# Written order for three engines in the last pass of a decode kernel's backward, with the stages that need new loads at the end of an item

## The chip, the core and the metric

The kernel runs on one core of one Trainium2 chip. The metric is the device time of one execution in microseconds (us); lower is better. The kernel before takes 2007.58 us, the median of three runs (2006.96 to 2015.45). The profiled execution has a span of 2011.2 us.

## The reference

Two layers are applied twice to a single token `x` of 1024 numbers, and the kernel returns the output and the gradients of everything (`jax.vjp`):

```python
x = x + A(layernorm(x), k_cache, v_cache, wq, wo)     # attention with a cache
x = x + B(layernorm(x), w1, b1, w2, b2)               # relu(h)**2 in between
x = x + A(layernorm(x), k_cache, v_cache, wq, wo)     # the same weights and caches
x = x + B(layernorm(x), w1, b1, w2, b2)
# in A: q = x @ wq in 32 heads; 8 heads share one of 4 groups of k and v, each 65536 x 128
#       p = softmax(q k^T / sqrt(128)); o = p v; o @ wo
```

All inputs and outputs are bfloat16. The caches are 67 MB each for k and for v, and their gradients, which sum over both uses of A, are as large. A gradient of k or v at one position is a sum of 16 outer products (8 heads, 2 layers).

## The kernel before, in words

The work goes through the caches in four passes: forward of the first attention, forward of the second, backward of the second (these three are `attn_fwd`, `attn_fwd` and `attn_bwd3`), and the last one, `attn_bwd4` (L1263), which does the backward of the first attention and writes the gradients of k and v for both. Between the passes lie the dense layers.

**Items and stages.** A pass walks over 256 items; an item is 8 columns of 128 cache rows in one of the 4 groups, in the order of `ITEMS[3]` (all items of a group, then the next group). Blocks of J = 32 columns, that is of 4 items and 1 MB, are what one DMA loads or stores. `pipeline` (L825) is a software pipeline: in step i it calls, for each entry of a list of stages, that stage's function for the item that is due by the stage's lag, then one step of background work (`bg.step`). The stages of the last pass are: `vT` takes a block of v from its load (`kv8`, which emits the load on SyncE where it is first asked for) and transposes 8 tiles on TensorE into a PSUM tile `ps_tr`, which `evac` (L150) copies to `kt`; the first seven blocks were kept transposed from the pass before. `vS` multiplies these by the output's gradient into `ps_sc` and, at the end of a block, VectorE multiplies that by the stored exponentials into `X` (L1367). `eIn` copies the exponentials of a block on GpSimd; `eT` and `xT` transpose the exponentials and `X` of a block (L1334). `dV8` and `dK8` make the gradients of v and k: `outer16` (L1382) has two products of two matmuls each into a PSUM tile `ps_gg` (L1390), evacuates each to a slot in `arena` (by `evac`, on ScalarE at L161 or VectorE at L164), and stores the full block from GpSimd's queue (L1396). `k8` takes a block of k from its load and accumulates the gradient of q in `ps_acc` (L1421).

**Buffers.** In this pass PSUM holds 2 buffers of `ps_tr`, 1 of `ps_sc`, 2 of `ps_gg` and 1 of `ps_acc`. SBUF has 20 slots of one block each (`arena`); 8 hold the exponentials of the four groups at the start and come free two by two, as a group ends. A load or a staging tile takes a slot when the code asks for it, and waits on the chip for that slot's last user, often a store.

**Background.** `Background` (L762) steps generators: `g_outer` and `g_outer_wide` make the weight gradients, each step one product into `ps_gg` (`rank2`, L1467) or its rows (`rows2`, L1452); `g_rowdots` (L562) loads two slabs of wo or wq, yields "wait" for eight steps, and then multiplies 8 rows on VectorE, one a step (L583), with a sum on ScalarE (L572).

**What sets the order.** The order in which Python emits instructions need not be the order on an engine. Outside of a region marked `tc.manual_schedule`, a scheduler reorders each engine's instructions by a simulation of when their inputs are ready. Inside such a region the named engines keep the written order; SyncE and GpSimd are still ordered by the scheduler. `ORDERED` (L981) names TensorE, VectorE and ScalarE, and the first three passes are already in such regions; the last one is not. `keep_in_program_order` pins a single instruction behind all that was emitted for its engine before it.

**The end.** At the last item `k8` calls `on4` (L1742), whose `else` branch does what is left: the product with wq (`PRE["rows"].run()`), the last layernorm's backward and the last weight gradient. Ten steps before the end `fill4` (L1761) transposes the last slabs of wq and drains the background.

Of the kernel before, what the change touches and what calls it, by code (L numbers as in the profile page):

```python
# [20 lines left out]
def kernel(  # L21
# [540 lines left out]
    def g_rowdots(slab_it, nk, vcol, nj, finish, name):  # L562
        n = nj * P
        y = vec.tile([P, nk], F32, name=name)
        nc.gpsimd.memset(y[:], 0.0)
        vbc = None
        due = None
        steps = 8 if PS["pass4"] else WAIT_STEPS

        def total(t, kc):  # L570
            def f():
                nc.scalar.activation(out=t[:, :], in_=t[:, :], func=ACTF.Copy, accum_out=y[:, kc:kc + 1])  # L572
            return f
        for kc, slab in slab_it:
            if vbc is None:
                vbc = yield from g_bcast_vec(vcol, nj)
                for _ in range(steps - WAIT_STEPS + 1):
                    yield "wait"
            elif kc % 4 == 0:
                for _ in range(steps):  # L580
                    yield "wait"
            t = mvs.tile([P, n], BF, name="mv_t", tag="mv_t", bufs=2)
            nc.vector.tensor_tensor(out=t[:, :], in0=slab, in1=vbc[:, :], op=ALU.mult)  # L583
            add_load(dve=0.1 + n * 0.00054, act=0.42 + n * 0.00083)
            if due is not None:
                due()
            due = total(t, kc)
            yield
        due()
        yield  # L590
        r = finish(y[:, :])
        if r is not None:
            yield from r
        yield


    class Rows:
# [227 lines left out]
    def pipeline(items, stages, bg, end=(), holds=(), lead=None):  # L825

        def due(lag):
            at = {}
            for k, it in enumerate(items):
                at.setdefault(k + lag + LEAD if lead is None or lag >= 0 else k + ~lag + lead(k), []).append(it)  # L830
            return at
        LEAD = 0 if lead is None else lead(len(items))
        when = [due(l) for _, l in stages]
        maxlag = max(l for _, l in stages) + LEAD
        for i in range(len(items) + maxlag):
            NOW["i"] = i
            NOW["wide"] = NOW["pairs"]
            for at, k in holds:
                if i == at:
                    hold(k)  # L840
            tasks(i - 0.5)
            for n, (fn, lag) in enumerate(stages):
                for it in when[n].get(i, ()):
                    fn(*it)
                if n == 0:
                    tasks(i)
            bg.step(max(0, i - LEAD))
            NOW["wide"] = False
            NOW["step"] += 1
            for before, fn in end:  # L850
                if i == len(items) + maxlag - before:
                    fn()
        while TASKS:
            k = min(TASKS)
            NOW["i"] = int(k + 0.5)
            tasks(k)
# [406 lines left out]
    def attn_bwd4(p, La, Lb, on_group, bg, stack, end=()):  # L1263
# [172 lines left out]
        for b in range(V_LEAD * 8 // J // 2):  # L1436
            nexts.append(("k",) + items[(b + 2) * J // 8])
            nexts.append(("v",) + items[(b + NKEEP[2]) * J // 8])
        pipeline(items, [(vT, ~0), (vS, ~TLEAD), (eIn, 0), (eT, TLEAD), (dV8, DV_LAG), (xT, DK_LAG - 1), (dK8, DK_LAG), (k8, B4_LAG)], bg,
                 end, lead=V_SHIFT)  # L1440

# [300 lines left out]
    def on4(g):  # L1742
        if g != lastg[3]:
            bg.add(g_dn(L1, dn1, g, g == firstg[3]))
            bg.normal.append(gwq(g))
        else:
            next(PRE["gwq"])
            PRE["rows"].run()
            next(PRE["gwq"])
            dxn1 = ln_bwd(dn1[:], L1["n"], L1["rstd"])  # L1750
            dx0 = tmp.tile([P, DC], F32, name="dx0")
            nc.vector.tensor_tensor(out=dx0[:], in0=dx1[:], in1=dxn1[:], op=ALU.add)
            col_to_dram(dx0, D, out_1.rearrange("a b d -> (a b d)"))
            run(PRE["gwq"])

    def last_v():

# [3 lines left out]
    def fill4():  # L1761
# [5 lines left out]
                                  lastg[3] * 1024)  # L1767
        next(PRE["gwq"])
    attn_bwd4(3, L1, L3, on4, bg, b4, [(12 + B4_LAG, last_v), (20, pre_load("wq4", lambda: wq_slabs(lastg[3], 2))), (10, fill4)])
    b4.close()  # L1770
    ps4_stack.close()

# [29 lines left out]
```

## Time and profile before

| | before |
|---|---|
| time, median of 3 | 2007.58 us |
| span of the profiled execution | 2011.2 us |
| TensorE busy | 1627.2 us (81%) |
| VectorE busy | 1171.7 us (58%) |
| ScalarE busy | 1045.1 us (52%) |
| GpSimd busy | 142.9 us (7%) |
| moved by DMA | 794.98 MB, mean 395 GB/s |
| granted TensorE clock, mean | 0.892 |

The last pass runs from about 1212 us to the end. Shares of busy time are means over stages with different limits; the busy time of TensorE is of pipelined matmuls with modelled ends, so it says little about how close TensorE is to its limit. The DMA share, by contrast, is near 1.00 in most of the span: a window with a full DMA share can't be shortened by anything but moving fewer bytes or moving them at a better rate. What ends a wait is named by the profile from semaphore events ("<-").

### The profile page before, as it was taken

The page shows a single profiled execution, that of the slowest core. Times are in us where ns is not written, and L with a number is a line of the kernel's source. Part 1 is how long each engine was busy: PE and PEld are TensorE (multiplying, and loading weights), DVE is VectorE, ACT ScalarE, POOL GpSimd, SP SyncE. Part 2 cuts the span into 40 slices and gives each one's busy share as a digit, 9 for nine tenths or more (in the row PEclk, how much of TensorE's full clock was granted, in tenths as well). Part 3 has the DMA queues.
Part 4 walks back from the last instruction along what each step waited for, and adds up shares of the span by engine and source line. Part 5 has one row for each costly group of instructions (what it writes and reads, how often), then busy time and mean ns, then how long its engine had stood idle before and what let it go on. Part 6 is the DMA issues. An engine that isn't in the chain of part 4 may idle for free. (4 is left out here: it accounts for less than half of the span.)

```text
span 2011.2 us, 67084 instructions
## 1 busy us (share of the span) xinstructions
PE 1627.2 (81%) x30228; PEld 1319.5 (66%) x30228; DVE 1171.7 (58%) x2426; ACT 1045.1 (52%) x1608; POOL 142.9 (7%) x332
## 2 busy tenths in 40 slices
PE   6877788687877777878787888788789799977887
PEld 6877777687777776767777785455455465644554
DVE  5645555255545544435454477656677677866775
ACT  3534344253433453426354365656678576756765
POOL 0000000000000000000000001111111111111211
PEclk9989999699999998899888999878898877888996
DMA  9999999999999998899999987998999999999996
GB/s 390 421 424 420 424 424 402 395 405 420 425 420 424 425 391 335 356 421 424 417 420 412 394 311 284 360 377 350 394 418 424 423 411 370 418 423 388 424 404 243
DMA packets 101037, 794.98 MB, mean 395 GB/s; under 512 B 9472, under 2 KB 9486, under 8 KB 37134
## 3 DMA queue, kind: packets, MB, share of 16 engines
q1 hardware_dynamic: 76670, 624.99, 76.2%
q0 software_dynamic: 24080, 165.70, 20.0%
q8 instruction: 236, 3.87, 0.8%
q14 instruction: 51, 0.42, 0.1%
HBM read 624.96 MB, written 165.69 MB: 393 GB/s over the span
## 5 line engine op out<-in xcount | busy, mean ns | idle before, releaser
L164 DVE COPY kt<-ps_tr 128x1024 bf16<-128x1024 bf16 x724 | 496.4, 688 | 489.8 <-PE ps_tr L1007 252.6
L161 ACT CAST arena<-ps_gg 128x1024 bf16<-128x1024 f32 x457 | 446.9, 1012 | 234.2 <-PE ps_gg L1390 161.6
L1007 PE MATMUL ps_tr<-ident_b,arena 128*128 128x128 bf16 x3840 | 306.9, 224 | 45.6 <-DMA arena<-in_A_k_cache_dram 33.3
L161 ACT COPY kt<-ps_tr 128x1024 bf16<-128x1024 bf16 x164 | 170.9, 1047 | 191.7 <-PE ps_tr L1199 113.5
L1007 PEld LDWEIGHTS <-arena 128*128 128x128 bf16 x3840 | 231.4, 100 | 54.1 <-DMA arena<-in_A_k_cache_dram 36.5
L1109 PE MATMUL ps_acc<-arena 128*128 128x64 bf16 (+4 forms) x4096 | 203.8, 195 | 67.5 <-DMA arena<-in_A_v_cache_dram 53.8
L164 DVE CAST arena<-ps_gg 128x1024 bf16<-128x1024 f32 (+2 forms) x186 | 222.2, 1195 | 61.5 <-PE ps_gg L1390 32.4
L1390 PE MATMUL ps_gg<-GG,xt 64*128 64x512 bf16 x1024 | 221.5, 433 | 21.5 <-ACT arena L161 13.1
L1319 PE MATMUL ps_tr<-ident_b,arena 128*128 128x128 bf16 x1824 | 186.6, 240 | 39.1 <-DMA arena<-in_A_v_cache_dram 37.7
L1109 PEld LDWEIGHTS <-arena 128*128 128x128 bf16 x4096 | 157.7, 100 | 73.2 <-DMA arena<-in_A_v_cache_dram 57.4
L1090 ACT ACTIVATE arena<-S_sb,L_negm 128x128 bf16<-128x128 f32 x256 | 165.5, 1003 | 62.4 <-DVE L_negm L1075 62.4
L1199 PE MATMUL ps_tr<-ident_b,arena 128*128 128x128 bf16 x1920 | 157.9, 229 | 43.8 <-DMA arena<-in_A_v_cache_dram 41.6
L1025 PE MATMUL ps_sc<-L_qpad,kt 128*128 128x64 bf16 (+7 forms) x3584 | 181.7, 193 | 14.2 <-ACT kt L161 6.6
L1319 PEld LDWEIGHTS <-arena 128*128 128x128 bf16 x1824 | 123.9, 107 | 98.0 <-issue 56.1
L1025 PEld LDWEIGHTS <-kt 128*128 128x128 bf16 x3584 | 151.2, 100 | 19.3 <-ACT kt L161 8.9
L1199 PEld LDWEIGHTS <-arena 128*128 128x128 bf16 x1920 | 119.8, 103 | 49.3 <-DMA arena<-in_A_v_cache_dram 44.7
L1421 PEld LDWEIGHTS <-arena 128*128 128x128 bf16 x2048 | 97.8, 105 | 73.4 <-issue 47.5
L1090 ACT ACTIVATION_READ_ACCUMULATOR arena<-S_sb,L_negm 128x1 f32 x256 | 128.1, 500 | 0.0
L1350 PEld LDWEIGHTS <-kt 128*128 128x128 bf16 x1824 | 86.5, 104 | 56.6 <-issue 55.7
L1350 PE MATMUL ps_sc<-DOB,kt 128*128 128x64 bf16 (+3 forms) x1824 | 119.1, 201 | 0.0
L1244 PE MATMUL ps_acc<-dsT,arena 128*128 128x64 bf16 (+7 forms) x2048 | 103.8, 195 | 14.0 <-DMA arena<-in_A_k_cache_dram 10.4
L1421 PE MATMUL ps_acc<-X,arena 128*128 128x64 bf16 (+3 forms) x1536 | 99.6, 203 | 15.7 <-DMA arena<-in_A_k_cache_dram 15.7
(292 smaller groups left out, 2160.7 us busy)
## 6 DMA issues: line engine op xcount, KB each, us to landing
arena<-in_A_k_cache_dram SPq DMA_DIRECT2D x86, 2048.0 KB, 21.3
arena<-in_A_v_cache_dram SPq DMA_DIRECT2D x83, 2048.0 KB, 21.1
out_dram<-arena POOLq DMA_DIRECT2D x149, 1024.0 KB, 10.4
arena<-in_A_v_cache_dram SPq DMA_DIRECT2D x76, 1024.0 KB, 11.7
arena<-in_A_k_cache_dram SPq DMA_DIRECT2D x76, 1024.0 KB, 11.4
arena<-in_B_w_dram SPq DMA_DIRECT2D x32, 896.0 KB, 7.9
arena<-in_A_wo_dram SPq DMA_DIRECT2D x22, 1024.0 KB, 13.6
arena<-in_A_wq_dram SPq DMA_DIRECT2D x20, 1024.0 KB, 14.5
```

The costliest lines, as they stand in the source:

```text
L161: nc.scalar.copy(out=out, in_=in_)
L164: nc.vector.tensor_copy(out=out, in_=in_)
L1007: nc.tensor.transpose(pt[:, i, :], kb8[:, i, :], ident_b[:, :])
L1025: nc.tensor.matmul(state["ps_s"][:, s:s + w, :].rearrange("p a b -> p (a b)"), lhsT=kt[:, i, :], rhs=L["qpad"][:, g, 0:w, :].rearrange("p ...
L1090: nc.scalar.activation(out=E(p, g, c0, SU)[:, :, h], in_=S[:, h, :], func=ACTF.Exp, bias=L["negm"][:, g, su, h:h + 1], scale=SCALE, accum_ ...
L1109: nc.tensor.matmul(ps_o[:, 0:w, :], lhsT=vb8[:, i, :], rhs=E(p, g, c, w), start=(c % SU == 0), stop=(c % SU == SU - 1), skip_group_check=True)
L1199: nc.tensor.transpose(pt[:, i, :], vb8[:, i, :], ident_b[:, :])
L1244: nc.tensor.matmul(ps_dq[:, 0:w, :].rearrange("p a b -> p (a b)"), lhsT=kb8[:, i, :], rhs=dsT[:, s:s + w, :].rearrange("p a b -> p (a b)") ...
L1319: nc.tensor.transpose(pt[:, i, :], vb8[:, i, :], ident_b[:, :])
L1350: nc.tensor.matmul(state["ps_dp"][:, s:s + w, :].rearrange("p a b -> p (a b)"), lhsT=vt[:, i, :], rhs=DOB[:, g, 0:w, :].rearrange("p a b - ...
L1390: nc.tensor.matmul(pg[:, 512 * h:512 * h + 512], lhsT=xt[64 * h:64 * h + 64, j1 // 8 + m, :], rhs=gg[64 * h:64 * h + 64, :, :].rearrange(" ...
L1421: nc.tensor.matmul(ps_dq[:, 0:w, :].rearrange("p a b -> p (a b)"), lhsT=kb8[:, i, :], rhs=X[:, s:s + w, :].rearrange("p a b -> p (a b)"), ...
```

## The change

The last pass is put into the written order on TensorE, VectorE and ScalarE, as the other passes are. The list of stages is reordered: those that need no new load come first in an item, and `vT` and `k8`, which need one, come last. (The list's first entry was also the point after which a step's tasks run; the last pass has none.) What followed the last item inside the region moves out of it, so that the scheduler still places it. The multiply of `g_rowdots` is pinned to its place in this pass. The purpose is that an engine which waits for a load has the item's other work behind it, not ahead of it, and that nothing is moved ahead on the strength of a simulated load time.

```diff
@@ g_rowdots
-            nc.vector.tensor_tensor(out=t[:, :], in0=slab, in1=vbc[:, :], op=ALU.mult)
+            ins = nc.vector.tensor_tensor(out=t[:, :], in0=slab, in1=vbc[:, :], op=ALU.mult)
+            if PS["pass4"]:
+                tc.keep_in_program_order(ins)
@@ attn_bwd4
-        pipeline(items, [(vT, ~0), (vS, ~TLEAD), (eIn, 0), (eT, TLEAD), (dV8, DV_LAG), (xT, DK_LAG - 1), (dK8, DK_LAG), (k8, B4_LAG)], bg,
-                 end, lead=V_SHIFT)
+        with tc.manual_schedule(engines=ORDERED):
+            pipeline(items, [(eIn, 0), (dV8, DV_LAG), (dK8, DK_LAG), (xT, DK_LAG - 1), (vS, ~TLEAD), (eT, TLEAD), (vT, ~0), (k8, B4_LAG)], bg,
+                     end, lead=V_SHIFT)
@@ on4: the else branch moves behind the call
-        else:
-            next(PRE["gwq"])
-            PRE["rows"].run()
...
-            run(PRE["gwq"])
...
     attn_bwd4(3, L1, L3, on4, bg, b4, [(12 + B4_LAG, last_v), (20, pre_load("wq4", lambda: wq_slabs(lastg[3], 2))), (10, fill4)])
+    next(PRE["gwq"])
+    PRE["rows"].run()
...
+    run(PRE["gwq"])
```

More of the change, by code (lines that the diff above doesn't have):

```diff
@@ L1745, in on4 @@
             bg.normal.append(gwq(g))
-        else:
-            next(PRE["gwq"])
-            PRE["rows"].run()
[L1749 to L1753, printed above, removed]
-            run(PRE["gwq"])
     def last_v():
@@ L1769 @@
     attn_bwd4(3, L1, L3, on4, bg, b4, [(12 + B4_LAG, last_v), (20, pre_load("wq4", lambda: wq_slabs(lastg[3], 2))), (10, fill4)])
+    next(PRE["gwq"])
+    PRE["rows"].run()
+    next(PRE["gwq"])
+    dxn1 = ln_bwd(dn1[:], L1["n"], L1["rstd"])
+    dx0 = tmp.tile([P, DC], F32, name="dx0")
+    nc.vector.tensor_tensor(out=dx0[:], in0=dx1[:], in1=dxn1[:], op=ALU.add)
+    col_to_dram(dx0, D, out_1.rearrange("a b d -> (a b d)"))
+    run(PRE["gwq"])
     b4.close()
```

## The prediction

> **What bounds the kernel now.** I first cut the last pass into three stages with the view of windows, because one average hides that they have different limits: the first group of heads, the other three groups, and the drain.
>
> ```profile
> 1212.00:1412.00 200.00, 162.87 (x1999) 100.50 (x1994) 132.36 (x248) 121.24 (x139) 33.31 (x64) 0.82 0.89 345
> 1412.00:1965.00 553.00, 475.93 (x5911) 298.54 (x5907) 391.54 (x698) 381.18 (x452) 96.31 (x180) 0.85 1.00 410
> 1965.00:2011.20 46.20, 34.08 (x357) 19.79 (x354) 24.35 (x47) 25.16 (x27) 7.60 (x12) 0.66 0.57 226
> ```
>
> The last three columns are the granted TensorE clock, the DMA share and GB/s. In the 553 us of the middle stage DMA is full, so nothing that only speeds up an engine can gain there. What can be won is DMA time that stood empty: 11% of 200 us (22 us) in the first group, and 43% of 46 us (20 us) in the drain, where the last products are made after the last load. So I looked next for the holes in DMA, in windows of 5 us. These are the deepest of the two groups of them that matter:
>
> ```profile
> 1285.00:1290.00 5.00, 5.00 (x64) 3.15 (x63) 4.67 (x7) 4.31 (x7) 1.17 (x3) 0.82 0.78 320
> 1290.00:1295.00 5.00, 4.43 (x61) 2.96 (x59) 4.78 (x9) 4.84 (x7) 1.01 (x3) 1.00 0.53 213
> 1355.00:1360.00 5.00, 5.00 (x49) 3.32 (x46) 3.75 (x6) 2.02 (x2) 0.62 (x1) 0.50 0.50 198
> ```
>
> Then the waits of TensorE from 1212 to 1990 us (total, times, longest):
>
> ```profile
> PE ps_tr L1319 <- DMA arena<-in_A_v_cache_dram: 37.7, 12, 8.9
> PE ps_acc L1421 <- DMA arena<-in_A_k_cache_dram: 23.7, 7, 5.8
> PE ps_gg L1390 <- ACT arena L161: 13.1, 19, 5.3
> PE ps_sc L1347 <- DVE arena L1367: 8.6, 4, 7.9
> PE ps_sc L1347 <- DVE X L1367: 7.6, 4, 6.0
> ```
>
> 61.4 us are waits for loads, as it must be where DMA is full. But 7.9 and 6.0 us are single waits for a VectorE product (L1367). The timeline of VectorE shows what held the first:
>
> ```profile
> 1269.54 1.23 DVE L164 CAST arena<-ps_gg 128x1024 bf16<-128x1024 f32 x1
> 1279.18 1.29 DVE L583 TENSOR_TENSOR mv_t<-arena,vbc 128x1024 bf16<-128x1024 bf16 x2 [8.42 <-DMA arena<-in_A_wo_dram]
> 1280.39 0.68 DVE L1367 TENSOR_TENSOR arena<-ps_sc,arena 128x512 bf16<-128x512 f32 x1
> ```
>
> A multiply of the background work stood ahead of L1367 and waited 8.42 us for its weights; TensorE waited behind it, no stores came, and the hole at 1280 to 1300 us followed. The same happened at 1830 us (7.02 us, for wq), with a hole at 1835 to 1845 us.
>
> [...] L1367 started after the late multiply. [...] the page has only 21.5 us of idle time ahead of the 1024 L1390.
>
> ```profile
> L161 ACT CAST arena<-ps_gg 128x1024 bf16<-128x1024 f32 x457 | 446.9, 1012 | 234.2 <-PE ps_gg L1390 161.6
> L1390 PE MATMUL ps_gg<-GG,xt 64*128 64x512 bf16 x1024 | 221.5, 433 | 21.5 <-ACT arena L161 13.1
> ```
>
> [...] after a wait of 5.06 us a pair of L1390 takes 0.61 us for some 5 us, then 0.39 again.
>
> ```profile
> 1571.69 0.39 PE L1319 MATMUL ps_tr<-ident_b,arena 128*128 128x128 bf16 x2 [5.06 <-DMA arena<-in_A_v_cache_dram]
> 1574.82 0.61 PE L1390 MATMUL ps_gg<-GG,xt 64*128 64x512 bf16 x2
> 1578.15 0.39 PE L1390 MATMUL ps_gg<-GG,xt 64*128 64x512 bf16 x2
> ```
>
> **The change, part by part.** No instruction of weight is added or removed; only places change, as the listing of the built orders shows.
>
> (1) The 48 multiplies keep their written place on VectorE, eight items after the call of their load; an item takes 2.9 us (5911 matmuls in 553 us, 30.9 an item: 7910 over 256 items), so 23 us later. In the listing the old order has them in clumps (two, then one evacuation, then another) ahead of an X product; the new one has one an item. This takes away the two blocks. Worth, in empty DMA time: 1280 to 1300 us has shares 0.92, 0.78, 0.53, 0.73, so 1.04 x 5 = 5.2 us; 1835 to 1845 has 0.81 and 0.83, so 1.8 us. Sum 7.0 us.
> The pin also adds a wait: if weights are late, X products, copies of v and evacuations queue behind the multiply, and TensorE waits for those. The weight loads stand on SyncE for stores first:
>
> ```profile
> SPq L350 <- DMA out_dram<-arena: 570.8, 94, 20.1
> SPq L447 <- DMA out_dram<-arena: 82.9, 12, 20.7
> ```
>
> 82.9/12 = 6.9 us each, then land in 8.8 us (wo) or 19.4 us (wq, median): 15.7 or 26.3 us against 23. So wo is in time and wq about 3 us late in the mean; six slabs of wq give 0 to 20 us of VectorE waiting. I take 0, since TensorE has load waits to lose in the same place, and keep 20 for the range.
>
> (2) Stage order. An item now starts with what needs no load (eIn, dV8, dK8, xT, vS, eT) and ends with vT and k8. A TensorE stuck on a load has then made that item's outputs already, so stores go on. Before, the gradients' matmuls are strewn among vT and k8. The holes that follow load waits: 1355 to 1370 us (shares 0.50, 0.82, 0.70: 4.9 us), 1375 to 1380 (0.5 us), 1405 to 1410 (1.4 us), 1670 to 1675 and 1680 to 1685 (0.5 and 2.0 us): 9.3 us. I take two thirds, 6.2 us: the next item's outputs are still behind the wait. Bounds: 0 and 9.3.
>
> (3) What the written order costs on TensorE. ps_gg has two buffers. The background's product (L1467) is at an item's end and the next item's two L1390 follow at once, so the second of these wants the bank that L1467 has just filled. In the listing 165 of 683 ps_gg tiles have under 0.4 us of TensorE work since their bank's last tile; in the old order 8 of 681, median 1.1 us. From the timeline: the evacuation starts 0.43 us after the product's start and the bank is written again 1.06 us after that: 1.49 us, where two pairs of 0.33 us each are there after 0.66. Wait 0.83 us; at the low clock about 0.58. With the low clock in 32% of the time (mean clock 0.84 over both stages, two levels 1 and 0.5): 165 x (0.68 x 0.83 + 0.32 x 0.58) = 124 us. Not all of it is new: before, the products are paced by the same evacuations; a window at full clock, 1540 to 1560 us, has 271 matmuls, 2.28 us an item, where TensorE's issue intervals sum to 1.92. That is 0.36 x 256 x 0.68 = 63 us paid already. New: about 61 us. It lies beside the 61 us of load waits and 16 us of L1347 that TensorE has now, so I cost it at nothing. Check by pace: full clock 1.92 + 165/256 x 0.83 = 2.45 us an item, low clock 3.5 (87 matmuls in 10 us at 1355 us) + 0.37 = 3.87; with 32% low 1/(0.68/2.45 + 0.32/3.87) = 2.78 us, still under DMA's 2.89; before, 2.57. The margin shrinks from 11% to 4%.
>
> (4) Start and drain. The 16 items of lead are now four blocks of vS with nothing between (2.17 us each in the old timeline), so the first stores come some 6 us later; the loads of that time fill DMA: 0 to +5 us, taken 0. In the drain, 64 transposes of wq come in one block and the rest of the pass after them; its end is left to the scheduler as before: 0 to +5, taken 0.
>
> Sum: 2007.6 - 7.0 - 6.2 = 1994.4, so 1994.
>
> **Rivals.** (B) TensorE becomes the bound. Each bank wait is idle time; if it keeps the low clock for half of the time instead of 32%, an item takes 1/(0.5/2.45 + 0.5/3.87) = 3.00 us, 0.11 over DMA: 28 us over 256 items, less the 7.0: 2029. For it: the margin of 4%, and long stretches at 0.50 with TensorE busy throughout (1355 to 1360 us). Against: fewer long waits, after which the clock falls. Late wq (20 us) would come to 2020 in the same direction. (C) The holes only move: few free slots in the first group make them, loads wait for stores as long as now. For it: 570.8 us of such waits; 2006. (D) The order also lifts the middle stage to 424 GB/s, the best of its windows: 553 x (1 - 410/424) = 18 us more, and all of the 9.3: 2007.6 - 7.0 - 9.3 - 18 = 1973. Against: share 1.00 already.
>
> **How the numbers follow.** A (1994) 0.42, B 0.33, C 0.16, D 0.09. A reaches past -0.5% (1997.5) in about 0.37 of its 0.42, so with D faster is 0.46; C and the edges of A and B give 0.19 for within 0.5%, B the rest, 0.35. The likeliest is A, 1994. The range goes from a little under D, 1968, to B with the wq waits half added and the start and drain at their worst, 2029 + 16 = 2045.
>
> **What would show it.** Step 1: no VectorE wait over 5 us at the multiply, no hole behind it. Step 2: DMA share of the first group over 0.92. Step 3: waits of L1390 for ACT L161 rise from 13 us to about 100 while waits for loads fall below 20. If the low clock takes over 40% of the pass or DMA falls under 0.97 in the middle stage, B holds and the prediction is wrong; if multiplies wait for wq, the cost in step 1 was.

## The result: slower, and the profile after

The changed kernel takes 2145.96 us (median of 4 runs, 2132.25 to 2154.23) against 2010.28 us for the kernel before in the same comparison: a ratio of 1.0666, with a 95% interval of 1.0604 to 1.0728. The forecast was 1994 us in a range of 1968 to 2045; the time lies outside it, on the side of rival B, and beyond what B gave.

The same three stages, in the view of windows of the kernel after (us of the window, busy time of TensorE, weight loads, VectorE, ScalarE and GpSimd, then granted TensorE clock, DMA share, GB/s):

```profile
1212.00:1412.00 200.00, 153.22 (x1598) 90.79 (x1598) 113.31 (x200) 105.81 (x124) 28.98 (x56) 0.66 0.80 306
1412.00:2096.00 684.00, 508.44 (x6314) 325.26 (x6313) 428.63 (x760) 405.16 (x483) 101.59 (x195) 0.80 0.89 347
2096.00:2142.70 46.70, 26.75 (x363) 16.55 (x360) 22.77 (x53) 20.02 (x22) 6.29 (x10) 0.79 0.45 177
```

The middle stage, full for DMA before (share 1.00), now has 0.89. The first group is emptier (0.80 against 0.89), and its clock fell from 0.82 to 0.66. The last stage is as long as it was. So nothing is lost in the drain: from 1212 us to 46 us before the end, the pass takes 884 us instead of 753, and these 131 us are nearly the whole loss of the span (2142.7 against 2011.2).

TensorE's waits in these 884 us (total, times, longest):

```profile
PE ps_gg L1392 <- ACT arena L161: 82.6, 138, 1.3
PE ps_gg L1455 <- DVE r_cc L1453: 32.7, 30, 1.9
PE ps_tr L1303 <- POOL CC L1301: 20.1, 11, 3.0
PE ps_gg L1392 <- ACT rowa L161: 14.5, 17, 1.1
PE ps_sc L1349 <- DVE X L1369: 11.0, 6, 9.9
```

No wait for a load is among TensorE's waits any more; there were 61 us. (The one of 9.9 us for X goes back to a load, as e17 below shows.) In their place the waits at L1392 (L1390 before; the two lines shown and the smaller ones) sum to 127 us, where they were 15. Of these, 116 are waits for a bank and 11 for `xt`, an operand that VectorE copies; the sums of this kind below, called bank waits, are counted in the same way, `xt` included. The second and third lines are of a kind that the prediction did not have: TensorE waits for operands made by VectorE (L1453, the casts for a background row) and by GpSimd (L1301, the copies for a coefficient's transposes). The page shows the same reversal in its groups: idle time ahead of the gradients' products was 21.5 us.

```profile
L161 ACT CAST arena<-ps_gg 128x1024 bf16<-128x1024 f32 (+2 forms) x445 | 429.8, 1002 | 262.3 <-PE ps_gg L1470 142.1
L1392 PE MATMUL ps_gg<-GG,xt 64*128 64x512 bf16 x1024 | 227.1, 457 | 134.4 <-ACT arena L161 85.0
```

The timeline of TensorE at full clock shows how they come about:

```profile
1591.28 0.41 PE L1470 MATMUL ps_gg<-rowb,rowa 2*128 2x512 bf16 x2
1591.62 0.39 PE L1392 MATMUL ps_gg<-GG,xt 64*128 64x512 bf16 x2
1592.79 0.39 PE L1392 MATMUL ps_gg<-GG,xt 64*128 64x512 bf16 x2 [0.78 <-ACT arena L161]
...
1595.03 0.53 PE L1455 MATMUL ps_gg<-ident_b,r_cc 128*2 128x128 bf16 x8 [0.84 <-DVE r_cc L1453]
...
1596.94 0.39 PE L1392 MATMUL ps_gg<-GG,xt 64*128 64x512 bf16 x2 [1.06 <-DVE rowa L164]
```

The background's product (L1470) and an item's two products stand side by side, so the third waits for the first one's bank, 0.78 us here and 0.62 us in the mean of some 190 such waits in 256 items. And a background row's matmuls (L1455) come right behind the casts that feed them in the code; VectorE gets to the casts late, and TensorE, which can no longer be given other work, waits for them.

To have one measure for all runs: I call 1212 us to 46 us before the end "the pass", and take the share of it at the low clock as twice what the mean granted clock lacks to 1, as the records have the two levels 1 and 0.5: of the windows of 1 us in the pass, 710 of 753 before and 837 of 884 after have exactly one of these, and none is under 0.50. Before: clock 0.85, 30% low. After: 0.77, 46% low. TensorE's idle time in the pass, summed from gaps in its timeline, rose from 111 to 221 us, its busy time from 639 to 662.

### The profile page after: what moved, and what is told of

Its sections match the earlier page's. It is cut to its first block, busy times and chain, and to the rows that moved or that the text cites. A ratio compares the mean times of both kernels' runs of the same rounds, so it can differ in the third digit from the quotient of the medians.

```text
span 2142.7 us, 67169 instructions
## 1 busy us (share of the span) xinstructions
PE 1657.9 (77%) x30228; PEld 1348.5 (63%) x30228; DVE 1185.3 (55%) x2414; ACT 1047.8 (49%) x1620; POOL 141.7 (7%) x332
## 3 DMA queue, kind: packets, MB, share of 16 engines
q8 instruction: 236, 3.87, 0.7%
## 5 line engine op out<-in xcount | busy, mean ns | idle before, releaser
L164 DVE COPY kt<-ps_tr 128x1024 bf16<-128x1024 bf16 x715 | 491.2, 688 | 462.2 <-PE ps_tr L1009 252.2
L161 ACT CAST arena<-ps_gg 128x1024 bf16<-128x1024 f32 (+2 forms) x445 | 429.8, 1002 | 262.3 <-PE ps_gg L1470 142.1
L1009 PE MATMUL ps_tr<-ident_b,arena 128*128 128x128 bf16 x3840 | 313.7, 227 | 41.0 <-DMA arena<-in_A_k_cache_dram 28.4
L164 DVE CAST arena<-ps_gg 128x1024 bf16<-128x1024 f32 (+1 forms) x198 | 241.4, 1220 | 166.9 <-PE ps_gg L1392 150.4
L1392 PE MATMUL ps_gg<-GG,xt 64*128 64x512 bf16 x1024 | 227.1, 457 | 134.4 <-ACT arena L161 85.0
L161 ACT COPY kt<-ps_tr 128x1024 bf16<-128x1024 bf16 x173 | 180.5, 1048 | 201.9 <-PE ps_tr L1201 116.7
L1009 PEld LDWEIGHTS <-arena 128*128 128x128 bf16 x3840 | 236.9, 102 | 50.7 <-DMA arena<-in_A_k_cache_dram 32.1
L1392 PEld LDWEIGHTS <-xt 64*128 64x128 bf16 x1024 | 53.2, 97 | 251.6 <-issue 214.8
L1111 PEld LDWEIGHTS <-arena 128*128 128x128 bf16 x4096 | 161.5, 101 | 65.3 <-DMA arena<-in_A_v_cache_dram 52.5
L1201 PE MATMUL ps_tr<-ident_b,arena 128*128 128x128 bf16 x1920 | 158.6, 230 | 43.2 <-DMA arena<-in_A_v_cache_dram 42.5
L1321 PE MATMUL ps_tr<-ident_b,arena 128*128 128x128 bf16 x1824 | 171.6, 250 | 14.3 <-DVE T L1305 4.9
L1201 PEld LDWEIGHTS <-arena 128*128 128x128 bf16 x1920 | 120.7, 103 | 47.7 <-DMA arena<-in_A_v_cache_dram 45.3
L1321 PEld LDWEIGHTS <-arena 128*128 128x128 bf16 x1824 | 135.1, 114 | 22.9 <-issue 22.9
L572 ACT ACTIVATE mv_t<-mv_t 128x1024 bf16<-128x1024 bf16 x96 | 101.7, 1061 | 9.3 <-DVE mv_t L583 9.2
L1352 PE MATMUL ps_sc<-DOB,kt 128*128 128x64 bf16 (+3 forms) x1824 | 105.0, 207 | 0.0
```

What stands on the lines that cost most here:

```text
L161: nc.scalar.copy(out=out, in_=in_)
L164: nc.vector.tensor_copy(out=out, in_=in_)
L1009: nc.tensor.transpose(pt[:, i, :], kb8[:, i, :], ident_b[:, :])
L1111: nc.tensor.matmul(ps_o[:, 0:w, :], lhsT=vb8[:, i, :], rhs=E(p, g, c, w), start=(c % SU == 0), stop=(c % SU == SU - 1), skip_group_check=True)
L1201: nc.tensor.transpose(pt[:, i, :], vb8[:, i, :], ident_b[:, :])
L1321: nc.tensor.transpose(pt[:, i, :], vb8[:, i, :], ident_b[:, :])
```

## The experiments

The theory after the result: TensorE sets the time now, by (a) waits for banks, (b) waits for producers that are written just ahead of their matmuls, (c) more time at the low clock. The rivals: the pinned multiplies are to blame (weights that come late), or the new order of stages is, or VectorE's and ScalarE's written order alone. Each of the 18 runs is set against runs of the kernel before on the same chip; their medians lie between 2007.5 and 2011.4 us, so the ratios compare better than the times. The columns from "pass" on are of one profiled execution, which need not be the median one: it took 2092 us in e9, 2022 in e17 and 2019 in e1. Idle is TensorE's.

| run | time, us | ratio (95%) | pass | TensorE busy | idle | clock | DMA share |
|---|---|---|---|---|---|---|---|
| before | 2010.28 | | 753 | 639 | 111 | 0.85 | 0.97 |
| after | 2145.96 | 1.0666 (1.0604 to 1.0728) | 884 | 662 | 221 | 0.77 | 0.87 |
| e1 pin only | 2013.06 | 1.0014 (0.9997 to 1.0031) | 759 | 624 | 132 | 0.85 | 0.96 |
| e2 order only | 2009.09 | 0.9979 (0.9963 to 0.9995) | 754 | 627 | 123 | 0.85 | 0.97 |
| e3 region, old order | 2042.23 | 1.0162 (1.0129 to 1.0196) | 792 | 637 | 152 | 0.84 | 0.94 |
| e7 without TensorE | 2090.77 | 1.0402 (1.0351 to 1.0453) | 831 | 667 | 162 | 0.80 | 0.91 |
| e8 TensorE only | 2059.31 | 1.0229 (1.0166 to 1.0292) | 799 | 606 | 192 | 0.84 | 0.94 |
| e4 products spread | 2121.99 | 1.0548 (1.0519 to 1.0577) | 855 | 702 | 152 | 0.76 | 0.89 |
| e9 producers early | 2083.06 | 1.0376 (1.0344 to 1.0408) | 832 | 633 | 198 | 0.82 | 0.92 |
| e11 spread, casts early | 2082.02 | 1.0359 (1.0327 to 1.0390) | 824 | 682 | 141 | 0.79 | 0.92 |
| e5 spread, all early | 2029.13 | 1.0097 (1.0066 to 1.0129) | 769 | 640 | 128 | 0.84 | 0.96 |
| e6 as e5, v first | 2030.62 | 1.0102 (1.0048 to 1.0155) | 773 | 650 | 122 | 0.83 | 0.96 |
| e10 after, filled | 2110.88 | 1.0509 (1.0475 to 1.0543) | 859 | 715 | 144 | 0.89 | 0.90 |
| e13 early, filled | 2060.59 | 1.0257 (1.0226 to 1.0289) | 799 | 681 | 118 | 0.93 | 0.94 |
| e16 as e5, filled | 2036.23 | 1.0117 (1.0084 to 1.0150) | 777 | 685 | 92 | 0.93 | 0.95 |
| e12 before, early | 2011.85 | 1.0010 (0.9988 to 1.0031) | 754 | 633 | 118 | 0.84 | 0.98 |
| e14 before, filled | 2003.85 | 0.9963 (0.9949 to 0.9976) | 746 | 679 | 65 | 0.93 | 0.98 |
| e15 order, filled | 2002.47 | 0.9953 (0.9941 to 0.9965) | 741 | 664 | 76 | 0.95 | 0.98 |
| e17 pin, X in halves | 2009.97 | 0.9997 (0.9979 to 1.0014) | 762 | 631 | 128 | 0.84 | 0.96 |
| e18 as e15, X in halves | 1998.95 | 0.9927 (0.9902 to 0.9951) | 741 | 666 | 73 | 0.95 | 0.98 |

### The parts alone: e1, e2, e3

e1 is the kernel before with the multiply pinned, nothing else; e2 is the kernel before with the new list of stages, its scheduler free; e3 is the changed kernel with the old list of stages.

```diff
 e1
+            ins = nc.vector.tensor_tensor(out=t[:, :], in0=slab, in1=vbc[:, :], op=ALU.mult)
+            if PS["pass4"]:
+                tc.keep_in_program_order(ins)
 e2
+        pipeline(items, [(eIn, 0), (dV8, DV_LAG), (dK8, DK_LAG), (xT, DK_LAG - 1), (vS, ~TLEAD), (eT, TLEAD), (vT, ~0), (k8, B4_LAG)], bg,
 e3
         with tc.manual_schedule(engines=ORDERED):
+            pipeline(items, [(vT, ~0), (vS, ~TLEAD), (eIn, 0), (eT, TLEAD), (dV8, DV_LAG), (xT, DK_LAG - 1), (dK8, DK_LAG), (k8, B4_LAG)], bg,
```

> The kernel before with only the pin of the background's multiply: the last pass still goes to the scheduler on all engines. Theory 1 (the written order on TensorE costs, through waits for the two ps_gg banks): the pin is harmless or helps a little, as forecast for step 1: the single VectorE waits of 8.4 and 7.0 us at the multiply go, 1995 to 2008 us. Theory 3 (the pinned multiply waits for late weights and holds VectorE): most of the loss appears here, over 2080 us.

> The kernel before with only the list of stages in the new order, no region and no pin. Theory 1: the scheduler spreads the products again, so within 1% of before, 1990 to 2030 us, and waits of the gradients' matmuls (L1390) for ScalarE stay near 13 us. Theory 4 (the new order of the stages itself is bad, since v and k are asked for last): at least half of the 136 us is here, over 2075 us.

> The changed kernel with the list of stages back in the old order (v first), still in the written order on three engines. Theory 1: still over 2090 us, since any written order with two products in a row and the background's product near them meets its own banks; waits of L1392 for evacuations stay over 80 us. Theory 4: near before, under 2040 us.

The pin does nothing that can be told (1.0014; its time lies above the 1995 to 2008 us that were expected), and the new order under the scheduler takes 0.2%: neither alone is the cause. The written order is, and the new list makes it worse: the same region with the old list costs 1.6% where the new one costs 6.7%. For e3 both theories missed: 2042 us is far below the 2090 of theory 1, and the waits fell, so the list matters more than it said. In e3 the background's product and an item's first product have `vT` and `vS` between them, and TensorE's waits for a bank at the gradients' products sum to 29 us instead of 127 (43 more at the background's own products).

### Which engine's order: e7, e8

The region names VectorE and ScalarE only (e7), or TensorE only (e8); the scheduler keeps the others.

```diff
-        with tc.manual_schedule(engines=ORDERED):
 e7
+        with tc.manual_schedule(engines={mybir.EngineType.DVE, mybir.EngineType.Activation}):
 e8
+        with tc.manual_schedule(engines={mybir.EngineType.PE}):
```

> The changed kernel with only VectorE and ScalarE in the written order; TensorE goes to the scheduler. Theory 1: TensorE spreads its products again, so at least two thirds of the 136 us come back: under 2055 us. If it stays over 2100 us, the order on VectorE and ScalarE is what holds TensorE.

> The changed kernel with only TensorE in the written order; VectorE and ScalarE go to the scheduler. Theory 1: nearly as slow as the changed kernel, over 2100 us, with the same waits of L1392 for its banks (over 90 us). If it is under 2050 us, the order on VectorE and ScalarE costs.

Both cost: 4.0% and 2.3%, which sum to nearly the 6.7% of all three. Neither came where it was expected: with e7 between the two forecasts and e8 far below the 2100 us of theory 1, the orders of VectorE and ScalarE count as well as TensorE's. What e7 pays with is not taken apart; its clock is 0.80, and TensorE waits 57 us at the gradients' products and 32 us for loads. e8 separates the two kinds of wait. Its bank waits at the gradients' products are those of the changed kernel (138 us), but with VectorE under the scheduler, which moves the casts ahead, the waits for producers fall from 53 to 3 us, and the clock stays at 0.84:

```profile
PE ps_gg L1392 <- ACT arena L161: 84.6, 138, 1.4
PE ps_sc L1349 <- DVE X L1369: 19.3, 11, 11.1
PE ps_gg L1392 <- DVE arena L164: 15.6, 28, 2.3
```

So bank waits of this size, at an unchanged clock, go with a pass longer by some 46 us (799 against 753), not by nothing; and they alone do not bring the low clock, which takes 31% here.

### Banks and producers: e4, e5, e6, e9, e11

e4 parts an item's two products: between them now stand `xT` and `vS`, and the background's step moves between `vT` and `k8`. e9 leaves the products alone and writes the producers earlier: the casts for a background row 3 steps ahead of their matmuls, the copies for a coefficient in the item before its transposes. e5 does both; e11 has the spread products and only the casts early; e6 is e5 with another list, which begins with `vT` and has the background's step at its end (other stages move too; `k8` stays last). The cut is shortened, and its comments are added here.

```diff
 e4
+ [(eIn, 0), (dV8, DV_LAG), (dK8, DK_LAG), (xT, DK_LAG - 1), (vS, ~TLEAD), (dV8b, DV_LAG), (dK8b, DK_LAG), (eT, TLEAD), (vT, ~0), (k8, B4_LAG)]
+ # dV8b, dK8b: the second product; bg.step between vT and k8
 e9 (and e5, e6); e11 only the casts
+                if j == 2 and a0 + 4 < nA:
+                    cc = casts(a_cols, (a0 + 4, a0 + 4))     # used three steps later by rows2
...
+        def eS(g, c8):                                       # a stage at TLEAD - 1
+            if c8 == sufirst[(g, c8 // SU)]:
+                su_setup(g, c8 // SU)                        # cf and the copies to CC
```

> The changed kernel with the same work in a spread order: the two products of dV8 or dK8 are parted by xT and vS, and the background step stands between vT and k8, so that between a bank's writing and its next use there are 1.2 to 1.4 us of matmuls instead of 0.66. Theory 1: the waits of L1392 for evacuations fall from 128 us to under 60 and the time falls by at least 60 us, to 2030 to 2080 us. If these waits fall but the time does not (over 2120 us), other waits of the written order or the low clock set the pace.

> The spread order of the run before, and the two other chains on which TensorE stood in it taken apart: the casts for the background's rows are emitted three steps before their matmuls (the first of each generator excepted), and the casts and GpSimd copies of a new score unit one item before their transposes. Theory 1b (TensorE's own waits in the written order, of whatever kind, set the pace of an item): its waits for these, 40 and 30 us in the spread order, fall under 25 us together, and the time falls by 40 us or more from 2122, to 2060 to 2085 us. Theory 2 (the low clock sets the pace): the waits fall but the share of the low clock stays at 45% and the time over 2100 us.

> The same as the run with both chains taken apart, but with v first in an item and the background's step last. Theory 1b: TensorE's waits are as few as there, and with the low clock's share of the old order in the region (33% against 45%) the time is under 2042 us (that run without spreading), perhaps under 2011. Theory 4 (with v last, its load is asked for late and the pace suffers): this run is faster than the one with v last by 50 us or more although TensorE's listed waits are alike. If both land within 15 us of each other, the place of v does not matter once the waits are gone.

> The written order as in the changed kernel, with one thing altered: the casts of the background rows and the copies ahead of a coefficient's transposes are emitted some steps before their matmuls; the two output products of an item still stand side by side. If what costs the time is the waits for producers that are emitted just ahead, this alone brings what it brought on top of the spread products (93 us): about 2053 us, and the share of the last pass at the low clock falls from 45% to about 32%. If the bank waits (128 us of TensorE's idle time) and these chains are to be removed together, as when each hides behind the other, about 2110 us and a low clock above 40%. If the sum of idle times is all that counts, 33 + 20 us less: about 2093 us.

> The written order with spread products (2122 us), and of the two early edits only the one on VectorE: the casts of the background rows 3 steps ahead of their matmuls. Both edits together gave 2029. By the idle time that they removed (40 us for the casts, 30 us for the copy on GpSimd) casts alone should give four sevenths of the 93 us: about 2069 us. If the copies on GpSimd are what counts (they wait 3 us at a time, the casts 1.9 us), 2100 us or more; if the casts are all of it, about 2035 us.

In e4 the bank waits at the gradients' products fall from 127 to 42 us and TensorE's idle time by 69, but the time only by 24 us. The freed time went into slower matmuls: busy time rises by 40 us, with the clock at 0.76. Then each early producer brings more: casts 40 us (e11), the copies another 53 (e5, below its 2060 to 2085), and the clock goes back to 0.84, near the 0.85 of the kernel before. TensorE's waits in e5, those for banks, for X and for the casts:

```profile
PE ps_gg L1500 <- ACT arena L161: 20.5, 49, 0.7
PE ps_sc L1363 <- DVE X L1383: 19.1, 11, 16.0
...
PE ps_gg L1410 <- ACT arena L161: 9.2, 23, 0.8
...
PE ps_gg L1485 <- DVE r_cc L1475: 7.5, 8, 1.5
```

The wait for GpSimd's copies has gone from the list, that for the casts fell from 32.7 to 7.5 us. Taken the other way round, early producers alone (e9) bring 63 us with the bank waits unchanged (134 us). The expectation of e9 had numbers for three theories (2053, 2110, 2093); at 2083 it is nearest to the sum of idle times and fits none well. The two cures are not additive: spreading is worth 1.2% before the producers are early (1.0666 to 1.0548) and 2.8% after (1.0376 to 1.0097). Together they take 1.0666 to 1.0097. With these waits gone, it makes no difference whether v comes first or late in an item, which was the purpose of the change: e5 and e6 are 1.0097 and 1.0102.

### The low clock: e10, e13, e16, e14, e15

If the low clock comes from the short idle stretches, work in these should bring the full clock back. e10 is the changed kernel with two matmuls of 448 columns, which nobody reads, ahead of each item's second product, into columns of the accumulator's bank that are not used.

```diff
+                if m and "ps_dq" in state:
+                    for _ in range(2):
+                        nc.tensor.matmul(state["ps_dq_w"][:, 64:512], lhsT=ident_b[:, :], rhs=gg[:, :, :].rearrange("p a b -> p (a b)")[:, 0:448],
+                                         start=True, stop=True, skip_group_check=True)
                 pg = ps_gg()
```

> The changed kernel, and ahead of the second output product of every item (where TensorE waits some 0.8 us for a bank) two matmuls of 448 columns that nobody reads, into columns of the accumulator's bank that nothing uses; the output is not changed. About 256 x 0.39 us = 100 us of extra work at the full clock, put where TensorE stands idle. If the low clock comes from these short idle stretches, its share falls from 45% towards 31% and the time from 2146 to 2070 to 2120 us although TensorE does more. If idle time has no part in the low clock (it follows the work, or the extra work brings more of it), the share stays at 45% or above and the time is 2150 to 2220 us.

The expectation was wrong in one thing: the fill with its start flag set does alter an output. The gradient of wq, which is made from the accumulator of this bank, is wrong in e10 (relative error 0.96). e13 to e16 and e18 have the fill with `start=False`, and there this output is right; what the flag does in the bank no run shows. No order and no amount of work depends on it. e10 itself was not run again in that form.

TensorE is busy 53 us more in e10, and the kernel is 35 us faster. The page's line of TensorE clocks (tenths, 40 slices) of after, then of e10:

```profile
PEclk9989997899999979998999867758699779869877
```

```profile
PEclk9999998799999989988999969899899899989988
```

The clock of the pass rises from 0.77 to 0.89: 46% at the low level become 22%. Nothing else was changed, so the fill brings the clock back. That it does so by ending idle stretches is one reading. The other is that it adds work to TensorE, over 128 rows where a product has 64: in e16 below the clock rises too, by 0.09, although few bank waits are left to fill (21 us at the gradients' products in e5), and e4 took 69 us of idle time away without a fill and the clock stayed low. No run tells the two apart.

Which waits go with the low clock can be read across the runs of the written order without a fill. The low share follows the number of TensorE's waits of 1.5 to 4 us, as counted in the traces: 21 in the kernel after, e4 and e11 (43 to 47% low), 11 in e7 (39%), 2 to 7 in e3, e5, e6, e8 and e9 (31 to 37%). The bank waits, nearly all of them shorter, do not order the runs: e8 has all of them and 31%, e4 a third and 47%. This is a pattern over nine runs and no proof; e10 keeps 17 such waits and has 22%.

The timeline of e10 shows the fill in its place, and what a wait that is not filled still does:

```profile
1588.99 0.39 PE L1396 MATMUL ps_gg<-GG,xt 64*128 64x512 bf16 x2
1589.32 0.55 PE L1392 MATMUL ps_acc<-GG,ident_b 128*128 128x448 bf16 x2
1589.80 0.39 PE L1396 MATMUL ps_gg<-GG,xt 64*128 64x512 bf16 x2
...
1593.30 0.52 PE L1303 MATMUL ps_tr<-ident_b,CC 128*128 128x128 bf16 x2 [2.55 <-POOL CC L1301]
...
1596.38 0.61 PE L1396 MATMUL ps_gg<-GG,xt 64*128 64x512 bf16 x2
1596.92 0.93 PE L1392 MATMUL ps_acc<-GG,ident_b 128*128 128x448 bf16 x2
1597.78 0.61 PE L1396 MATMUL ps_gg<-GG,xt 64*128 64x512 bf16 x2
```

With the fill the second product follows with no gap. After the wait of 2.55 us for GpSimd's copies a pair of products takes 0.61 us instead of 0.39, the fill 0.93 instead of 0.55.

e13 puts the fill into e9 (early producers), e16 into e5 (few bank waits left for the fill to lie in), e14 into the kernel before, e15 into e2.

> The written order with early casts and copies (2083 us, low clock in 36% of the last pass), and the fill of the earlier run, two matmuls of 448 columns that nobody reads ahead of an item's second output product. The bank waits stay where they are. If the waits for late producers and the low clock explain what the written order costs, both are gone here and the time comes near the spread version's 2029 us: 2025 to 2050 us, low clock under 20%. If the place of the two products side by side costs by itself, the fill takes 36 us as before at most: 2047 to 2075 us. If the fill only buys clock where the chains stand idle too, 2083 us or more.

> The written order with spread products and early producers (2029 us, TensorE busy 640 us and idle 128 us of the last pass of 769 us) and the fill ahead of the second product. No bank wait is there for the fill to lie in, so its 100 us are work added. If the written order is still bound by TensorE, they lengthen it, less what the clock gives back (low clock 32%, all of it worth some 70 us): 2040 to 2070 us. If the last 20 us over the kernel before are the low clock's, 2005 to 2020 us.

> The kernel before with the same fill, its scheduler free. It waits for loads (DMA share 0.97 in the last pass, low clock in 30%). If the loads bound it whatever the clock, the time stays within 0.5%: 2000 to 2020 us, with a smaller share of the low clock. If the low clock costs it time, below 1998 us. If the 100 us of extra work on TensorE do not fit beside the loads, above 2020 us.

> The kernel before with the new list of stages, its scheduler free, and the fill. Each of the two alone gave 0.9979 and 0.9963 of the kernel before. If both gains come from work that TensorE can do while a load is late, they add: about 0.994, 1998 us. If the loads are the floor that both reach, 0.996 as with the fill alone, 2003 us.

e13 falls by 22 us against e9, to a low share of 14% (clock 0.93), and stays 2.6% over the kernel before. So late producers and the low clock do not explain all. Products side by side cost by themselves: e16, with the same fill and the same clock but the products apart, is at 1.0117, 1.4% less. In e16 the fill brings the clock from 0.84 to 0.93 and the time does not fall (1.0117 against 1.0097, within both intervals): the clock gives back what the fill adds. So the last 1% of e5 is not told apart by it; both numbers of that expectation missed. One wait of 16.0 us in e5 is for X, which itself waited 17.8 us for a load of wo.

e14 shows what bounds the kernel before. The fill takes its low share from 30% to 14% and the time by 0.37% only. Its waits for loads, in the view of waits:

```profile
PE ps_sc L1347 <- DVE X L1367: 26.0, 2, 15.4
PE ps_tr L1319 <- DMA arena<-in_A_v_cache_dram: 15.7, 5, 6.6
```

Waits for loads fall from 61 to 16 us, and the DMA share only goes from 0.97 to 0.98: so its loads bound it at either clock. The two waits for X in the first line are again X products that waited for weights, as in e17 below. e15, with the new list of stages on top, is at 0.9953 (0.9941 to 0.9965) of the kernel before; what the list adds to the fill is within the intervals.

### The same producers under the scheduler: e12

The early casts and copies of e9 in the kernel before, with its scheduler.

```diff
+        pipeline(items, [(eS, TLEAD - 1), (vT, ~0), (vS, ~TLEAD), (eIn, 0), (eT, TLEAD), (dV8, DV_LAG), (xT, DK_LAG - 1), (dK8, DK_LAG), (k8, B4_LAG)], bg,
```

> The kernel before, its scheduler left as it is in the last pass, with only the early casts and early copies. The scheduler moves such producers ahead by itself, so nothing is left to gain: 2004 to 2014 us. If the kernel before also loses time to them, below 2000 us.

Nothing (1.0010), while the same edit takes 63 us off in the written order. This fits the scheduler's having done it: TensorE's waits in the kernel before have none for these casts and copies.

### What X waits for: e17, e18

The kernel after has one block of VectorE on weights left, longer than either of before:

```profile
DVE X L1369 <- DMA arena<-in_A_wo_dram: 10.8, 1, 10.8
```

It is not a multiply that waits there. The timeline of VectorE has no L583 ahead of it:

```profile
1506.23 1.23 DVE L164 CAST arena<-ps_gg 128x1024 bf16<-128x1024 f32 x1 [2.12 <-PE ps_gg L1392]
1518.22 0.69 DVE L1369 TENSOR_TENSOR X<-ps_sc,arena 128x512 bf16<-128x512 f32 x1 [10.77 <-DMA arena<-in_A_wo_dram]
```

X reads exponentials, which no load of weights brings. But it reads them as one view of two planes, one for each layer, and slots between the planes are loaded with weights once a group has ended. Two X products end such a wait in the kernel before, for 7.0 us (wq) and 2.1 us (wo). e17 is e1 with the product made in two halves, one for each plane (the copies of `eIn` likewise). e18 is e15 with the same halves.

```diff
-                nc.vector.tensor_tensor(out=split2(X[:, :, :]), in0=split2(ps_dp[:, :, :]), in1=E2(g, c0, J), op=ALU.mult)
+                for l in range(2):
+                    nc.vector.tensor_tensor(out=X[:, :, l * R:(l + 1) * R], in0=ps_dp[:, :, l * R:(l + 1) * R], in1=E(l, g, c0, J), op=ALU.mult)
```

> The kernel before with the multiply pinned, and the product X = scores x stored exponentials made in two halves, one for each layer's plane of exponentials (the copies of eIn likewise). One view over both planes spans the slots between them, into which weights are loaded after a group has ended; the halves do not. If X waits for weights only by that span, its waits for loads of wo and wq (12.7 us in the pin alone, 9.1 in the kernel before) are gone, and with them the second of the two blocks that the prediction wanted to remove for 7.0 us: 2000 to 2006 us. If the loads bind elsewhere at once, within 0.2% of the kernel before. If 64 more VectorE instructions (some 0.1 to 0.2 us each, 10 us) cost more than the blocks, above 2014 us.

> The fastest so far (the new list of stages under the scheduler, with the fill: 0.9953 of the kernel before) with X in halves as well. If the blocks of X are idle time that the loads do not make up for, 0.990 to 0.993, about 1992 us; if the loads are its floor, 0.994 to 0.997.

In e17 VectorE waits for no load of weights at all, neither at the multiply nor at X, and the time is that of the kernel before: 0.9997 (0.9979 to 1.0014). The expectation put the 64 more VectorE instructions at 0.1 to 0.2 us each; in the trace of before, casts of only 128x4 (L1450) take 0.15 to 0.17 us. The first lines of TensorE's waits in e17, all for loads:

```profile
PE ps_tr L1321 <- DMA arena<-in_A_v_cache_dram: 47.5, 10, 10.8
PE ps_acc L1425 <- DMA arena<-in_A_k_cache_dram: 41.3, 9, 12.5
```

They sum to 89 us. In e1, the same kernel with X whole, loads are 88 us and X another 12.5, in the kernel before 61 and 16; e1 and e17 were profiled in slower executions than the kernel before, so these sums do not show where X's wait went. So X waited only by the span of its view. Taking both blocks away is worth 0.2% at most by the interval, less than the 7.0 us (0.35%) of the prediction. e18 has the lowest ratio of all, 0.9927 (0.9902 to 0.9951), near what was expected if the blocks did cost; but its interval meets that of e15, so the halves are not shown to add to it.

## Why the prediction was wrong

**Step 1, the pin: one block misread, and both worth less than reckoned.** The step gave 7.0 us for the two blocks. The first, 8.42 us at the multiply, does go: in e1 and in the kernel after no multiply waits for weights, and the step's cost of 0 to 20 us did not occur there either. But "The same happened at 1830 us (7.02 us, for wq)" was not the same. That wait stood at X itself, with no multiply ahead of it, in the kernel before:

```profile
1822.81 0.69 DVE L164 COPY kt<-ps_tr 128x1024 bf16<-128x1024 bf16 x1 [0.71 <-PE ps_tr L1319]
1830.52 0.69 DVE L1367 TENSOR_TENSOR X<-ps_sc,arena 128x512 bf16<-128x512 f32 x1 [7.02 <-DMA arena<-in_A_wq_dram]
```

It came by X's view over two planes, and the pin cannot touch it (in e1 it is 11.2 us, in the kernel after 10.8 us, on wo). Nor are the blocks worth what the empty DMA time behind them says: e17 has neither, and gains nothing that can be told (0.9997). Here an emptier window of DMA was not time lost; that later loads make up for it fits, but no run shows it.

**Step 2, stores that go on: no case for it left.** It was to bring 6.2 us by stores during load waits of TensorE. In the kernel after TensorE has no load wait, so there is nothing to overlap. Its sign, a DMA share over 0.92 in the first group, did not come (0.80). Under the scheduler the new list is worth 0.2% (e2). e6 against e5 says that the place of v in an item does nothing in the written order either.

**Step 3: the sum right, the cost wrong.** This is the step that failed. The waits at L1392 were put at 124 us and measured 127. That the sum is so near is in part luck: 165 waits of 0.75 us in the mean were reckoned, and 187 of 0.62 us for a bank came, with 11 us for `xt`. But "It lies beside the 61 us of load waits and 16 us of L1347 that TensorE has now, so I cost it at nothing" fell in three ways.

First, too much of it was called "paid already". The step took 63 of the 124 us as old, so that 61 new ones lay under 77 us of waits that could go. But the waits at L1390 in the pass were 15 us before, and the prediction's own line has 21.5 us of idle time for all of L1390. So some 112 us were new. The load waits did go (61 to 0), those for L1367 hardly (16 to 13); once the waits that can go are gone, every further microsecond is added. By this reckoning, which is an estimate, 112 - 61 - 3 = 48 us are left over; e8, which has the bank waits and almost none of the late producers, pays 46 us of pass.

Second, the pace of an item started too low, by the same allowance. It was put at 2.45 us at the full clock and 3.87 at the low one; measured between successive groups of `k8` of one speed, it is about 2.75 and 4.05. The step had started from 1.92 us of issue where the kernel before took 2.28 us at full clock; 2.28 + 0.53 = 2.81 is near what was measured. The late producers are not in this difference: items of the kernel after with no such wait have a median of 2.73 us, and e8 and e9, which have few of these waits, 2.8. They come on top, 53 us in 41 waits, and had no term at all. The listing of the built orders, from which the step took the distance between two uses of a bank, was asked about banks only. e9 takes 41 of these 53 us away and gains 63.

Third, the low clock. The check by pace kept the share that it had, 32%. It became 46%. With the step's own item times that alone is 1 / (0.54/2.45 + 0.46/3.87) = 2.95 us, 0.06 over DMA's 2.89 and 15 us in 256 items; with the measured item times it is 1 / (0.54/2.75 + 0.46/4.05) = 3.23 us, 0.34 over and 86 us. The other 45 of the 131 us lie where this pairing does not look: in the start (step 4), and between items with a set-up or a change of clock; how they divide was not measured.

**Rival B had the right bound, with too small a size.** TensorE became the bound. B's signs came: low clock over 40% (46%), DMA under 0.97 in the middle stage (0.89). So did those of step 3, which hold as well where it costs something: waits of L1390 for ScalarE at about 100 us (82.6 for L161 into `arena`, 97 with `rowa`), load waits under 20 (0). B took half of the time at the low clock, near the truth, but 2.45 and 3.87 us an item, and so 3.00 us and 2029 us. B's reason for the low clock, the bank waits, is not shown. In the kernel after, the low share is 46% while the longest bank wait is 1.3 us; but with as many bank waits (138 us against 127) e8 has 31%, so that in this kernel they bring the low clock at most together with the other waits. Against B the prediction argued "fewer long waits, after which the clock falls". The trace of before has such a case at 1571.69 us, where the granted clock went from 1.00 to 0.50 in the wait of 5.06 us and stayed there for some 6 us. But load waits of up to 8.9 us did go (61 us to 0), and the low share rose from 30 to 46%.

The end of the range does not follow from its words either: half of the 20 us for wq and 5 us each for start and drain are 20 us, not 16. The measured time is beyond both.

**Step 4: the drain right, the start too small.** The last 46 us and the time up to 1212 us are unchanged. But the step had the first stores "some 6 us later" and took 0. The first output product comes 15 us later, and the first store that follows it too (1235.7 us instead of 1220.9). Before, then after:

```profile
1214.70 0.39 PE L1390 MATMUL ps_gg<-GG,xt 64*128 64x512 bf16 x1
1230.00:1250.00 20.00, 16.77 (x220) 10.74 (x220) 14.89 (x26) 11.41 (x13) 3.98 (x8) 0.83 0.70 279
```

```profile
1229.99 0.61 PE L1392 MATMUL ps_gg<-GG,xt 64*128 64x512 bf16 x2
1230.00:1250.00 20.00, 15.47 (x109) 6.22 (x109) 9.13 (x10) 11.90 (x13) 3.42 (x6) 0.50 0.38 157
```

The four blocks of `vS` ahead of it run mostly at the low clock (mean 0.54 from 1212 to 1230 us, where it was 1.00) and wait 0.8 us for VectorE between them, so each takes about 3.1 us and not 2.17. Nor do the loads of that time fill DMA: its share is 0.68 in these 18 us, where it was 0.85, and 0.38 in the next 20 us, where it was 0.70. Whether these 15 us are all lost is open: e5 starts 13 us late too and has made a quarter of its products by 1412.5 us, before the 1423.7 of the kernel before.

## What to carry to other kernels

Before an engine's order is fixed by hand, look at each of its matmuls for two distances in that order: to the last use of its bank and to the producer of its operands on another engine; what a scheduler had moved apart can come back as a wait, here 187 times for a bank and 41 times for a producer in 256 items. A wait moved from one cause to another is free only up to the idle time that the bound leaves (here, by the estimate above, for 64 of 112 new us); what counts as paid already has to stand in the list of waits of the kernel before. The pace per item is to be reckoned from the measured pace, with a term for each kind of wait and for a lower clock, which the busy time of the matmuls shows (639 us before, 662 after) and the list of waits does not.

## What was not expected of the hardware

The longest waits are no measure of the low clock. The kernel before has single load waits of up to 8.9 us and 30% of the pass at the low clock; the kernel after has bank waits of 1.3 us at most and producers' waits of 3.0 us at most, one wait of 9.9 us for X, and 46%. With the fill, 53 us more of busy time, the share was 22% (e10), and in the kernel before the same fill took it from 30% to 14% (e14). That work which nobody reads makes a kernel faster, by 35 us in e10 and by 0.37% in e14, was not foreseen before these runs.
